# Scores a chunk ahead, values of the dilated heads first, seven products from chunk 3, and one x tile per row

## The chip, the core and the metric

The kernel runs on one core of a Trainium2 chip. A core has TensorE for matrix products, VectorE, ScalarE and GpSimd for element-wise work, a SyncE queue (SP) that issues most transfers, and 16 DMA engines behind the queues. The time is device microseconds from start to end of one launch; it is given as the median of several runs. A profile is taken of one execution by the hardware; its span runs from the first to the last instruction.

## What is computed

The inputs are q, k and v of shape (8, 8, 576, 64): 8 batch rows, 8 heads, 576 positions, 64 channels, in float32. Each row goes through attention with two masks, and the result through a feed-forward block:

```python
scores = (1 / sqrt(64)) * q @ k.T
rel = pos[:, None] - pos[None, :]
mask_plain = (rel >= 0) & (rel < 32)                        # heads 0 to 3, "sliding"
mask_dil = (rel >= 0) & (rel < 128) & (rel % 4 == 0)        # heads 4 to 7, "dilated"
attn = softmax(where(mask, scores, -1e9))
x = (attn @ v)  ->  (4608 tokens, 512)                      # 8 rows of 576 tokens
h = x @ w_in                                                # 512 -> 2048
out = relu(h) ** 2 @ w_out                                  # 2048 -> 512, float32
```

## The kernel before

**Two units of work.** Attention is done by batch row: eight rows b = 0 to 7 of 576 tokens. The feed-forward block is done by chunk: nine chunks c = 0 to 8 of 512 tokens (chunk 0 takes 576, chunk 1 the 448 behind them). A chunk is `mm1` (16 blocks of 128 of the 2048 inner columns; each is four accumulated matmuls over the 512 input columns, then a relu on ScalarE into `rt`; VectorE squares two blocks at a time into `g`) and then `mm2` (g times w_out). All is in float16 with float32 accumulation.

**The plain mm2 and the seven products.** `mm2_gen` runs 4 token blocks of 16 matmuls, 512 columns wide. `seven_gen` computes the same product of a chunk with seven products of half-size blocks instead of eight, 112 matmuls of 256 columns; it needs sums of parts of g (`S1` to `S3`, made on VectorE behind mm1 by `sums_behind` and once more in the products), sums of parts of w_out (`T1` to `T4`, made once by `sum_w_out_gen` in eight VectorE subtractions), and seven VectorE additions or subtractions at the end. Before, chunks 1 to 3 take the plain form and chunks 4 to 8 the seven products; the T sums are made during chunk 2.

**A row's attention** is cut into steps, named in `row_parts`: `s0`, `s1` scores of the sliding heads and `z0`, `z1` of the dilated heads (TensorE, then two exps on ScalarE, then one multiply by the mask on VectorE into `AT`); `a0` to `a2` values of the sliding heads and `d0`, `d1`, `e0`, `e1` of the dilated heads (eight small matmuls AT times v, then a reciprocal and a multiply on VectorE); `x0`, `x1`, `y0`, `y1` transposes of the result on TensorE and a ScalarE copy into `xT`, from which mm1 reads. The scores and values steps use four PSUM banks as two pairs in turn, the chunk's matmuls the other four.

**The order is written by hand.** A chunk is a generator with 64 steps (32 in mm1; 32 in the plain mm2, 28 in the seven products). `run` advances it and inserts the row's parts at given steps: "24:s0" puts s0 behind step 24. Each engine works its instructions in the order of the program. In chunk c the program works on row b = c + 1. Before, chunks 1 and 2 hold the scores of row b at steps 24 to 36 and its values at 40 to 60; chunk 3 holds the scores and values of row 4 at 2 to 20 and 24 to 44, and the scores of row 5 at 47 to 59; chunks 4 and 5 hold the values of row b at 2 to 32 and the scores of the row behind it at 36 to 54; chunk 6 the values of row 7.

**How a row's data come.** Ahead of chunk c the program issues, for row b + 1: on GpSimd a `see` (a one-element copy that waits until row b's `QKTp` has landed), two loads `n` (q and k of the sliding heads, cast to float16 on the way) and two `dd` (dilated heads, to a DRAM buffer); then the copy `o` of n into token order (`in_token_order`, 128 x 2304 elements). On SP: two transposing DMAs from dd into `QKTd`, two stores of o into a DRAM buffer `dp`, two transposing DMAs from dp into `QKTp`, and the loads of v: six of `sv` (sliding heads) and two of `sd` (dilated heads). GpSimd then casts row b's v from sv and sd into `vp` and `vd` (`cast_v`: three casts and four). sv and sd exist once, QKTp, QKTd, vp and vd twice, xT has room for three rows.

**xT** is one tile with a ring of three rows:

```python
RING = 3 * S
xT = const.tile([P, NDM, RING], FP16, name="xT")
```

`x_sliding` and `x_dilated` write row b at place b % 3, and `mm1_tile` reads 512 tokens from place t0 % RING, in two matmuls where the ring ends. That is so in chunk 3 (192 + 320) and in chunk 6 (384 + 128).

Of the kernel before, what the change touches and what calls it, by code (L numbers as in the profile page):

```python
# [8 lines left out]
FP16 = mybir.dt.float16  # L9
# [4 lines left out]
P = 128  # L14
# [3 lines left out]
def kernel(  # L18
# [9 lines left out]
    nc = tc.nc  # L28
# [56 lines left out]
        return b if dt == FP32 else b.bitcast(dt)  # L85


    RING = 3 * S
    xT = const.tile([P, NDM, RING], FP16, name="xT")


    WI = ((0, 512), (512, 1024), (1024, 2048))
# [60 lines left out]
    def load_sliding_v(b, m0=0, m1=NB):  # L153
        for m in range(m0, m1):
            lo = QB * m - PADP
            p0 = PADP if m == 0 else 0
            nc.sync.dma_start(
                out=sv[p0:P, m, :, :],
                in_=v[b, 0:HH, lo + p0 : lo + P, :].transpose([1, 0, 2]),
            )  # L160

    def load_dilated_v(b, t):
        vv = v[b, HH:H].rearrange("h (i c) d -> i h (c d)", c=DIL)
        if t:
            nc.sync.dma_start(out=sd[:, 1, :, :], in_=vv[QD - PADD : CL])
        else:
            nc.sync.dma_start(out=sd[PADD:P, 0, :, :], in_=vv[0:QD])

    def load_v(b):
        load_sliding_v(b)  # L170
        for t in range(2):
            load_dilated_v(b, t)

    def load_w_in(t):
        f0, f1 = WI[t]
# [24 lines left out]
    def cast_sliding_v(b, mp):  # L200
        m = 2 * mp
        nc.gpsimd.tensor_copy(vp[b % 2][:, m : m + 2, :, 0:D], sv[:, m : m + 2, :, :])  # L202

    def cast_dilated_v(b, t, a):
        c = 2 * a
        nc.gpsimd.tensor_copy(  # L206
            vd[b % 2][:, t, c : c + 2, :, 0:D],
            sd[:, t, :, D * c : D * (c + 2)].rearrange("p h (c d) -> p c h d", d=D),
        )

    def cast_v(b):
        for mp in range(NB // 2):
            cast_sliding_v(b, mp)
        for t in (0, 1):
            for a in range(2):
                cast_dilated_v(b, t, a)

# [7 lines left out]
            )  # L225
        return d

    def in_token_order(b, n):
        o = natp.tile([P, 9, HH, D], FP16, name=f"o{b}", tag="o")
        nc.gpsimd.tensor_copy(o, n.rearrange("p h j d -> p j h d"))  # L230
        return o

    def keep_sliding_qk(b, o):
# [18 lines left out]
    def mm1_tile(ffc, t0, t1, rt):  # L252
        w = t1 - t0
        ph = bank()
        o = t0 % RING
        cut = min(w, RING - o)
        for dmk in range(NDM):
            for a, b, x in ((0, cut, o), (cut, w, 0)):
                if a < b:
                    nc.tensor.matmul(  # L260
                        ph[:, a:b],
                        w_in_of(dmk, ffc),
                        xT[:, dmk, x : x + b - a],
                        start=(dmk == 0 and a == 0),
                        stop=(dmk == NDM - 1 and b == w),
                    )
            if dmk == 1:
                yield
        nc.scalar.activation(rt, ph[:, 0:w], ACTF.Relu)  # L269
# [394 lines left out]
    def x_sliding(b, half, xs, wide):  # L664
        px = pt(wide)
        for m3 in range(3):
            m = 3 * half + m3
            x = xs[m // 2][:, m % 2].rearrange("p h d -> p (h d)")
            for c in range(2):
                nc.tensor.transpose(  # L670
                    px[:, 288 * c + QB * m3 : 288 * c + QB * (m3 + 1)],
                    x[:, P * c : P * (c + 1)],
                    ident[0:QB, 0:QB],
                )
        t0 = (b % 3) * S + 288 * half
        nc.scalar.copy(  # L676
            xT[:, 0:2, t0 : t0 + 288],
            px[:, 0:UW].rearrange("x (c t) -> x c t", c=2),
        )

    def x_dilated(b, t, xs, wide):
        py = pt(wide)
        for a in range(2):
            for e in range(2):
                x = xs[a][:, e].rearrange("p h d -> p (h d)")
                for c in range(2):
                    o = 288 * c + QD * (2 * a + e)
                    nc.tensor.transpose(  # L688
                        py[:, o : o + QD],
                        x[0:QD, P * c : P * (c + 1)],  # L690
                        ident[0:QD, 0:QD],
                    )
        t0 = (b % 3) * S + 288 * t
        nc.scalar.copy(
            xT[:, 2:4, t0 : t0 + 288].rearrange("x c (i r) -> x c i r", r=DIL),
            py[:, 0:UW].rearrange("x (c r i) -> x c i r", c=2, r=DIL),
        )

# [199 lines left out]
    for t in range(2):  # L898
        for a in range(2):
            cast_dilated_v(1, t, a)  # L900
    o = in_token_order(2, n)
    transpose_dilated(2, dd)
    transpose_sliding(2, keep_sliding_qk(2, o))
    pending.append(mm2_by_rows_gen(0))
    parts = row_parts(1, True)
    parts.update(
# [7 lines left out]
            "4:t0 6:t1 8:s0:u0 10:s1:u1 12:z0 14:z1 18:a0 19:a1 20:a2 21:x0 22:d0 23:x1"  # L914
            " 24:d1 25:e0 26:e1 27:y0 28:y1",
            parts,
        )
    )
    load_v(2)

    rows_ = {b: row_parts(b, b > 3) for b in range(2, B)}
    SCORES = "{}:s0 {}:s1 {}:z0 {}:z1"
    VALUES = "{}:a0 {}:a1 {}:a2 {}:x0 {}:d0 {}:x1 {}:d1 {}:e0 {}:e1 {}:y0 {}:y1"
    for c in range(1, NTOKC):
        b = c + 1
        if b + 1 < B:
            see(QKTp[b % 2][0:1, 0, 0, PADP : PADP + 1])  # L930
            n, dd = load_whole_sliding_qk(b + 1), keep_dilated_qk(b + 1)
            o = in_token_order(b + 1, n)
            transpose_dilated(b + 1, dd)
            transpose_sliding(b + 1, keep_sliding_qk(b + 1, o))
        if b < B:
            cast_v(b)
        if b + 1 < B:
            load_v(b + 1)
        pending.append(moe_gen(c) if c < 4 else moe_seven_gen(c))
        plans, more = [], []  # L940
        if c < 3:
            plans.append((SCORES.format(*range(24, 40, 4)), rows_[b]))
            plans.append((VALUES.format(*range(40, 62, 2)), rows_[b]))
        if c == 2:
            it = sum_w_out_gen()
            more = [(4 + 7 * i, lambda it=it: next(it)) for i in range(8)]
        if c == 3:
            plans.append((SCORES.format(2, 8, 14, 20), rows_[b]))
            plans.append((VALUES.format(*range(24, 46, 2)), rows_[b]))
            plans.append((SCORES.format(47, 51, 55, 59), rows_[b + 1]))  # L950
        if 3 < c < B - 1:
            plans.append((VALUES.format(2, 5, 8, 11, 13, 16, 18, 22, 26, 29, 32), rows_[b]))
        if 3 < c < B - 2:
            plans.append((SCORES.format(36, 42, 48, 54), rows_[b + 1]))
        run(*plans, more=more)


# [28 lines left out]
```

## Time and profile before

| | |
|---|---|
| median of 3 runs | 312.45 us (312.25 to 313.09) |
| the profiled execution | 313.25 us, span 311.2 us |
| granted TensorE clock | 1.0 |
| TensorE busy | 297.2 us, 95% of the span, 2932 matmuls |
| VectorE busy | 198.2 us, 64% |
| ScalarE busy | 161.8 us, 52% |
| GpSimd busy | 85.4 us, 27% |
| starts of chunks 1 to 8 in the span | 65.6, 96.3, 128.6, 163.4, 194.9, 226.5, 255.5, 281.6 us |

In the profile PE is TensorE, DVE VectorE, ACT ScalarE, POOL GpSimd and SP the SyncE queue; L260 is a line of the kernel as printed above. L260 is mm1, L301 the plain mm2, L396 the seven products, L588 and L602 the scores, L641 and L655 the values, L670 and L688 the transposes, L676 and L694 the copies into xT. The chain of waits is followed back from the last instruction; each piece has its start in the span, its length, and the engine and line. A view by windows gives the busy time of each engine in a stretch of the span. In the timeline the bracket behind an instruction is the idle time of its engine ahead of it and what ended that.

### The profile page before, as it was taken

The page shows a single profiled execution, that of the slowest core. Times are in us where ns is not written, and L with a number is a line of the kernel's source. Part 1 is how long each engine was busy: PE and PEld are TensorE (multiplying, and loading weights), DVE is VectorE, ACT ScalarE, POOL GpSimd, SP SyncE. Part 2 cuts the span into 40 slices and gives each one's busy share as a digit, 9 for nine tenths or more (in the row PEclk, how much of TensorE's full clock was granted, in tenths as well). Part 3 has the DMA queues.
Part 4 walks back from the last instruction along what each step waited for, and adds up shares of the span by engine and source line. Part 5 has one row for each costly group of instructions (what it writes and reads, how often), then busy time and mean ns, then how long its engine had stood idle before and what let it go on. Part 6 is the DMA issues. An engine that isn't in the chain of part 4 may idle for free.

```text
span 311.2 us, 7133 instructions
## 1 busy us (share of the span) xinstructions
PE 297.2 (95%) x2932; PEld 200.7 (65%) x2932; DVE 198.2 (64%) x354; ACT 161.8 (52%) x286; POOL 85.4 (27%) x120
## 2 busy tenths in 40 slices
PE   3988999899999999999999999999999999999995
PEld 3657954455555555687545578657888885685584
DVE  6545645835852986297345879686868753863674
ACT  2646857278536772686356653565456406504610
POOL 5591027132703913283350344006000000000000
PEclk9999999999999999999999999999999999999999
DMA  7999989699979999998938894886120020012012
GB/s 117 242 205 212 213 185 234 156 227 206 224 180 220 266 196 164 248 235 166 236 134 185 162 216 122 190 173 141 67 71 3 2 101 34 2 46 91 0 36 101
DMA packets 75376, 46.73 MB, mean 150 GB/s; under 512 B 54416, under 2 KB 71056, under 8 KB 75152
## 3 DMA queue, kind: packets, MB, share of 16 engines
q1 hardware_dynamic: 67952, 32.52, 44.4%
q0 software_dynamic: 7248, 13.63, 24.7%
q8 instruction: 23, 0.38, 0.5%
q10 hardware_dynamic: 144, 0.13, 0.1%
q14 instruction: 9, 0.07, 0.1%
HBM read 39.85 MB, written 16.52 MB: 181 GB/s over the span
## 4 chain that ended last, share of the span: by engine, by line
PE 92%; DVE 2%; DMA 2%; ACT 2%; issue 1%; POOL 0%; DVEq 0%; POOLq 0%
PE PS L260 41%; PE PS L396 20%; PE PS L301 17%; PE PS L655 3%; PE PS L588 2%; PE PS L641 2%; PE PS L602 2%; DMA nd<-in_q_dram 2%; PE PS L688 1%; PE PS L670 1%; PE PS L523 1%; DVE AT L573 1%; ACT AT L569 1%; PE PS L581 1%; DVE x_p L627 1%
## 5 line engine op out<-in xcount | busy, mean ns | idle before, releaser
L260 PE MATMUL PS<-xT,wi 128*128 128x512 f16 (+6 forms) x768 | 136.1, 329 | 2.9 <-ACT xT L676 1.7
L269 ACT ACTIVATE rt<-PS 128x512 f16<-128x512 f32 (+2 forms) x160 | 88.7, 555 | 66.8 <-PE PS L260 64.0
L260 PEld LDWEIGHTS <-wi 128*128 128x128 f16 x768 | 79.2, 114 | 42.1 <-issue 3.0
L294 DVE TENSOR_TENSOR g<-rt 128x1024 f16<-128x1024 f16 (+1 forms) x64 | 47.6, 747 | 38.5 <-ACT rt L269 38.4
L301 PE MATMUL PS<-wo,g 128*128 128x512 f16 x256 | 64.4, 379 | 0.0
L569 ACT ACTIVATE AT<-PS 128x576 f16<-128x576 f32 x64 | 38.4, 650 | 19.8 <-PE PS L602 12.1
L396 PEld LDWEIGHTS <-S 128*128 128x128 f16 x320 | 31.0, 98 | 3.8
L301 PEld LDWEIGHTS <-g 128*128 128x128 f16 x256 | 21.3, 97 | 18.2
L396 PE MATMUL PS<-T,S 128*128 128x256 f16 x240 | 28.2, 273 | 0.0
L573 DVE TENSOR_TENSOR AT<-AT,maskp 128x1152 f16<-128x1152 f16 x14 | 15.0, 1072 | 19.1 <-ACT AT L569 19.1
L202 POOL CAST vp<-sv 128x512 f16<-128x512 f32 x24 | 20.6, 874 | 23.6 <-DMA sv<-in_v_dram 23.6
L206 POOL CAST vd<-sd 128x512 f16<-128x512 f32 x32 | 23.7, 773 | 10.5 <-DMA sd<-in_v_dram 10.4
L396 PEld LDWEIGHTS <-g 128*128 128x128 f16 x240 | 23.0, 98 | 3.2
L627 DVE TENSOR_TENSOR x_d<-PS,rcp_d 72x512 f16<-72x512 f32 x32 | 22.0, 687 | 1.1
L230 POOL COPY o<-n 128x2304 f16<-128x2304 f16 x6 | 13.0, 2172 | 30.6 <-issue 29.4
L396 PE MATMUL PS<-wo,g 128*128 128x256 f16 x160 | 19.5, 273 | 0.0
L676 ACT COPY xT<-PS 128x576 f16<-128x576 f16 x16 | 10.2, 637 | 14.6 <-PE PS L670 14.5
L573 DVE TENSOR_TENSOR AT<-AT,maskd 128x1152 f16<-128x1152 f16 x14 | 12.8, 917 | 7.3 <-ACT AT L569 7.3
L627 DVE TENSOR_TENSOR x_p<-PS,rcp_p 96x512 f16<-96x512 f32 x24 | 16.5, 687 | 0.8
L655 PEld LDWEIGHTS <-AT 128*128 128x128 f16 x256 | 12.4, 102 | 7.0 <-DVE x_d L627 1.3
L311 ACT COPY ot<-PS 128x512 f32<-128x512 f32 x16 | 9.4, 587 | 14.4 <-PE PS L301 14.4
L283 DVE TENSOR_TENSOR g<-rt 128x288 f16<-128x288 f16 x32 | 9.9, 309 | 9.9 <-ACT rt L269 9.8
(86 smaller groups left out, 257.3 us busy)
## 6 DMA issues: line engine op xcount, KB each, us to landing
sv<-in_v_dram SPq DMA_DIRECT2D x40, 128.0 KB, 4.0
out_dram<-c SPq DMA_DIRECT2D x19, 256.0 KB, 2.5
sd<-in_v_dram SPq DMA_DIRECT2D x8, 512.0 KB, 12.2
out_dram<-ot SPq DMA_DIRECT2D x15, 256.0 KB, 12.2
dp<-o SPq DMA_DIRECT2D x12, 288.0 KB, 3.8
sd<-in_v_dram SPq DMA_DIRECT2D x8, 288.0 KB
wo<-in_moe_w_out_dram POOLq DMA_DIRECT2D x4, 512.0 KB, 13.7
n<-in_k_dram POOLq DMA_DIRECT2D x6, 288.0 KB, 5.8
```

The costliest lines, as they stand in the source:

```text
L202: nc.gpsimd.tensor_copy(vp[b % 2][:, m : m + 2, :, 0:D], sv[:, m : m + 2, :, :])
L206: nc.gpsimd.tensor_copy(vd[b % 2][:, t, c : c + 2, :, 0:D], sd[:, t, :, D * c : D * (c + 2)].rearrange("p h (c d) -> p c h d", d=D),)
L230: nc.gpsimd.tensor_copy(o, n.rearrange("p h j d -> p j h d"))
L260: nc.tensor.matmul(ph[:, a:b], w_in_of(dmk, ffc), xT[:, dmk, x : x + b - a], start=(dmk == 0 and a == 0), stop=(dmk == NDM - 1 and b == w),)
L269: nc.scalar.activation(rt, ph[:, 0:w], ACTF.Relu)
L294: nc.vector.tensor_mul(g[:, f2 : f2 + 2, o:TOKC], rt[:, :, o:TOKC], rt[:, :, o:TOKC])
L301: nc.tensor.matmul(po, g[:, ffc, o + t * P : o + (t + 1) * P], w_out_of(ffc), start=(ffc == 0), stop=(ffc == NFF - 1),)
L396: nc.tensor.matmul(po[t], lhs(j)[:, t * P : (t + 1) * P], rhs(j), start=j == 0, stop=j == HF - 1)
L569: nc.scalar.activation(AT[:, u + i, 0:UW], ps[:, :, 0 : UW // 2], ACTF.Exp, scale=scale)
L573: nc.vector.tensor_mul(AT[:, u : u + n, 0:UW], AT[:, u : u + n, 0:UW], mask.unsqueeze(1).to_broadcast([P, n, UW]),)
L627: nc.vector.tensor_tensor(out=x[0:w], in0=pv[:, :, :, 0:D], in1=rcp[0:w].unsqueeze(3).to_broadcast([w, 2, HH, D]), op=ALU.mult,)
L655: nc.tensor.matmul(pav[:, e, h * (D + 2) : h * (D + 2) + D + 1], AT[:, 4 + 2 * a + t, off : off + P], vd[b % 2][:, t, 2 * a + e, h, 0 : D ...
```

## The change

It has five parts.

1. xT becomes three tiles, one for each place. `mm1_tile` now cuts a chunk wherever it crosses from one row to the next, not only at the ring's end: chunks 2 to 7 are cut (128 + 384, 192 + 320, 256 + 256, 320 + 192, 384 + 128, 448 + 64).
2. Chunk 3 takes the seven products too, and the T sums are made during chunk 1.
3. From row 4 on all four scores steps of a row come in the chunk in front, dilated heads first; row 3's scores and values come earlier in chunk 2; the values of rows 4 to 7 begin with the dilated heads, and in chunk 3 they lie at every third step.
4. From row 4 on, v of the dilated heads is loaded and cast first, and the casts of row b's v stand ahead of the o copy of row b + 1 on GpSimd.
5. The o copy of row 2 moves from GpSimd to ScalarE, at step 17 of chunk 0's mm2; the DMAs behind it are issued there too.

```diff
-    RING = 3 * S
-    xT = const.tile([P, NDM, RING], FP16, name="xT")
+    xT = [const.tile([P, NDM, S], FP16, name=f"xT{r}") for r in range(3)]
...
-    def load_v(b):
-        load_sliding_v(b)
+    def load_v(b, dilated_first=False):
+        if not dilated_first:
+            load_sliding_v(b)
         for t in range(2):
             load_dilated_v(b, t)
+        if dilated_first:
+            load_sliding_v(b)
...
-    def cast_v(b):
-        for mp in range(NB // 2):
-            cast_sliding_v(b, mp)
+    def cast_v(b, dilated_first=False):
+        if not dilated_first:
+            for mp in range(NB // 2):
+                cast_sliding_v(b, mp)
         for t in (0, 1):
             for a in range(2):
                 cast_dilated_v(b, t, a)
+        if dilated_first:
+            for mp in range(NB // 2):
+                cast_sliding_v(b, mp)
...
-    def in_token_order(b, n):
+    def in_token_order(b, n, eng=nc.gpsimd):
         o = natp.tile([P, 9, HH, D], FP16, name=f"o{b}", tag="o")
-        nc.gpsimd.tensor_copy(o, n.rearrange("p h j d -> p j h d"))
+        copy(eng, o, n.rearrange("p h j d -> p j h d"))
         return o
...
     def mm1_tile(ffc, t0, t1, rt):
         w = t1 - t0
         ph = bank()
-        o = t0 % RING
-        cut = min(w, RING - o)
+        rows_in = [(r, max(t0, r * S), min(t1, (r + 1) * S)) for r in range(t0 // S, (t1 - 1) // S + 1)]
         for dmk in range(NDM):
-            for a, b, x in ((0, cut, o), (cut, w, 0)):
-                if a < b:
-                    nc.tensor.matmul(
-                        ph[:, a:b],
-                        w_in_of(dmk, ffc),
-                        xT[:, dmk, x : x + b - a],
-                        start=(dmk == 0 and a == 0),
-                        stop=(dmk == NDM - 1 and b == w),
-                    )
+            for r, a, b in rows_in:
+                nc.tensor.matmul(
+                    ph[:, a - t0 : b - t0],
+                    w_in_of(dmk, ffc),
+                    xT[r % 3][:, dmk, a - r * S : b - r * S],
+                    start=(dmk == 0 and a == t0),
+                    stop=(dmk == NDM - 1 and b == t1),
+                )
...
-    o = in_token_order(2, n)
-    transpose_dilated(2, dd)
-    transpose_sliding(2, keep_sliding_qk(2, o))
+
+    def turn_row_2():
+        transpose_dilated(2, dd)
+        transpose_sliding(2, keep_sliding_qk(2, in_token_order(2, n, nc.scalar)))
+
     pending.append(mm2_by_rows_gen(0))
...
+        more=[(17, turn_row_2)],
...
-    rows_ = {b: row_parts(b, b > 3) for b in range(2, B)}
+    SEVEN = 3
+    rows_ = {b: row_parts(b, b > SEVEN) for b in range(2, B)}
     SCORES = "{}:s0 {}:s1 {}:z0 {}:z1"
     VALUES = "{}:a0 {}:a1 {}:a2 {}:x0 {}:d0 {}:x1 {}:d1 {}:e0 {}:e1 {}:y0 {}:y1"
+    SOON = "{}:z0 {}:z1 {}:s0 {}:s1"
+    EARLY = "{}:d0 {}:d1 {}:e0 {}:y0 {}:e1 {}:a0 {}:y1 {}:a1 {}:a2 {}:x0 {}:x1"
+    LATER = (EARLY.format(2, 5, 8, 11, 13, 16, 19, 21, 24, 27, 30), SOON.format(36, 42, 48, 54))
+    PLANS = {
+        1: (SCORES.format(*range(24, 40, 4)) + " " + VALUES.format(*range(40, 62, 2)), ""),
+        2: (
+            SCORES.format(8, 14, 20, 26) + " " + VALUES.format(*range(30, 52, 2)),
+            SOON.format(52, 56, 59, 62),
+        ),
+        3: (
+            EARLY.format(8, 11, 14, 17, 19, 22, 24, 27, 30, 33, 36),
+            SOON.format(40, 45, 50, 55),
+        ),
+        4: LATER,
+        5: LATER,
+        6: (LATER[0], ""),
+    }
     for c in range(1, NTOKC):
         b = c + 1
         if b + 1 < B:
             see(QKTp[b % 2][0:1, 0, 0, PADP : PADP + 1])
             n, dd = load_whole_sliding_qk(b + 1), keep_dilated_qk(b + 1)
+        if 3 < b < B:
+            cast_v(b, True)
+        if b + 1 < B:
             o = in_token_order(b + 1, n)
             transpose_dilated(b + 1, dd)
             transpose_sliding(b + 1, keep_sliding_qk(b + 1, o))
-        if b < B:
+        if b <= 3:
             cast_v(b)
         if b + 1 < B:
-            load_v(b + 1)
-        pending.append(moe_gen(c) if c < 4 else moe_seven_gen(c))
-        plans, more = [], []
-        if c < 3:
-            plans.append((SCORES.format(*range(24, 40, 4)), rows_[b]))
-            plans.append((VALUES.format(*range(40, 62, 2)), rows_[b]))
-        if c == 2:
+            load_v(b + 1, b + 1 > 3)
+        pending.append(moe_gen(c) if c < SEVEN else moe_seven_gen(c))
+        more = []
+        if c == 1:
             it = sum_w_out_gen()
-            more = [(4 + 7 * i, lambda it=it: next(it)) for i in range(8)]
-        if c == 3:
-            plans.append((SCORES.format(2, 8, 14, 20), rows_[b]))
-            plans.append((VALUES.format(*range(24, 46, 2)), rows_[b]))
-            plans.append((SCORES.format(47, 51, 55, 59), rows_[b + 1]))
-        if 3 < c < B - 1:
-            plans.append((VALUES.format(2, 5, 8, 11, 13, 16, 18, 22, 26, 29, 32), rows_[b]))
-        if 3 < c < B - 2:
-            plans.append((SCORES.format(36, 42, 48, 54), rows_[b + 1]))
-        run(*plans, more=more)
+            more = [(2 + 3 * i, lambda it=it: next(it)) for i in range(8)]
+        now, ahead = PLANS.get(c, ("", ""))
+        run((now, rows_.get(b)), (ahead, rows_.get(b + 1)), more=more)
```

More of the change, by code (lines that the diff above doesn't have):

```diff
@@ L674, in x_sliding @@
                 )
-        t0 = (b % 3) * S + 288 * half
+        t0 = 288 * half
         nc.scalar.copy(
-            xT[:, 0:2, t0 : t0 + 288],
+            xT[b % 3][:, 0:2, t0 : t0 + 288],
             px[:, 0:UW].rearrange("x (c t) -> x c t", c=2),
@@ L692, in x_dilated @@
                     )
-        t0 = (b % 3) * S + 288 * t
+        t0 = 288 * t
         nc.scalar.copy(
-            xT[:, 2:4, t0 : t0 + 288].rearrange("x c (i r) -> x c i r", r=DIL),
+            xT[b % 3][:, 2:4, t0 : t0 + 288].rearrange("x c (i r) -> x c i r", r=DIL),
             py[:, 0:UW].rearrange("x (c r i) -> x c i r", c=2, r=DIL),
@@ L916 @@
             parts,
-        )
+        ),
+        more=[(17, turn_row_2)],
     )
     load_v(2)
-    rows_ = {b: row_parts(b, b > 3) for b in range(2, B)}
+    SEVEN = 3
+    rows_ = {b: row_parts(b, b > SEVEN) for b in range(2, B)}
     SCORES = "{}:s0 {}:s1 {}:z0 {}:z1"
     VALUES = "{}:a0 {}:a1 {}:a2 {}:x0 {}:d0 {}:x1 {}:d1 {}:e0 {}:e1 {}:y0 {}:y1"
+    SOON = "{}:z0 {}:z1 {}:s0 {}:s1"
[10 more added lines that the diff above has]
+            SOON.format(40, 45, 50, 55),
+        ),
+        4: LATER,
+        5: LATER,
+        6: (LATER[0], ""),
+    }
     for c in range(1, NTOKC):
```

## Prediction, made before the result was known

> **What bounds the kernel now.** I read the page first, then the chain of waits in order of time, then the windows by chunk, and last the timeline of each place where the chain leaves TensorE. The page's busy rows and the head of its chain:
>
> ```profile
> PE 297.2 (95%) x2932; PEld 200.7 (65%) x2932; DVE 198.2 (64%) x354; ACT 161.8 (52%) x286; POOL 85.4 (27%) x120
> PE 92%; DVE 2%; DMA 2%; ACT 2%; issue 1%; POOL 0%; DVEq 0%; POOLq 0%
> ```
>
> TensorE is busy 95% and carries 92% of the chain, at a granted clock of 1.0. So a gain is either TensorE work that goes away or one of the few places where it stands still. From the chain in order of time, three kinds of line price the work:
>
> ```profile
> 126.90 1.73 PE PS L301 x8
> 269.35 12.23 PE PS L396 x112
> 154.20 0.36 PE PS L588 x12
> 154.56 1.83 PE PS L301 x8
> 204.41 1.73 PE PS L260 x8
> 236.15 1.75 PE PS L260 x16
> ```
>
> Eight 512-wide matmuls take 1.73 us (0.2166 each), so 64 take 13.86, for mm1 and for the plain mm2 alike; the seven products of a chunk take 12.23. One scores step takes 0.36, and the eight matmuls behind it 1.83 instead of 1.73, so 0.47 in all, and four take 1.88. A values step (8 or 6 matmuls) adds 0.25 to 0.26 between its neighbours, eleven 2.8. The last two lines are mm1 of chunk 5 (whole) and chunk 6 (each 512 cut into 384+128 where the ring wraps): 0.02 more for eight pairs. With these prices the chunks come out: chunk 2 13.86+13.86+1.88+2.8 = 32.4, and the chain has 32.3 (96.27 to 128.6); chunk 4 13.86+12.23+1.88+2.8 = 30.8 against 31.4; chunk 5 30.8 against 31.6; chunk 3 with eight score steps 14.0+13.9+3.8+2.8 = 34.5 against 34.8. What is left over in 3, 4 and 5 are waits, and row 1's values in chunk 0 hold another. The timeline (start, duration, engine, line):
>
> ```profile
> 53.62 2.11 POOL L230 COPY o<-n 128x2304 f16<-128x2304 f16 x1 [1.22 <-DMA n<-in_q_dram]
> 54.07 2.27 DVE L573 TENSOR_TENSOR AT<-AT,maskd 128x1152 f16<-128x1152 f16 x1 [0.94 <-ACT AT L569]
> 57.23 0.43 PE L641 MATMUL PS<-vp,AT 128*128 128x65 f16 x8 [1.09 <-DVE x_p L627]
> 178.34 0.38 PE L260 MATMUL PS<-xT,wi 128*128 128x512 f16 x1
> 179.24 1.24 PE L260 MATMUL PS<-xT,wi 128*128 128x512 f16 x5 [0.51 <-ACT xT L694]
> 210.66 1.46 PE L260 MATMUL PS<-xT,wi 128*128 128x512 f16 x6 [0.73 <-ACT xT L694]
> ```
>
> The mask multiply that takes 0.76 at 52.36 takes 2.27 beside GpSimd's copy, and a2 waits behind it. In chunks 4 and 5 a matmul of mm1 waits for the copy of y0, which writes the next row, a row that this chunk does not read.
>
> **Row 2's o copy on ScalarE (chunk 0, step 17).** Removed: the 2.27 beside the copy; the multiply goes back to 0.76 and ends at 54.83, so x of a0 (0.20+0.69 and gaps) is there at 55.95 instead of 57.17. a1 starts at 55.29 and steps follow each other by 0.69, so a2 starts at 55.98 instead of 57.23. Then VectorE's pace (0.93 a step) binds: x of a1 56.89, of a2 57.82, d0 at 57.85 instead of 58.90. I take -1.05. Added: one ScalarE copy of 2304 elements. The rows 288 (0.410), 448 (0.546) and 576 (0.650) give 0.83 ns an element on 0.17, so 2.1 us as an estimate (those read PSUM; the copy reads SBUF). It starts when the exps end (54.03) and n has landed (53.62), ends near 56.1, and the next ScalarE work, x0's copy, comes at 57.3: hidden by 1.2 us. Behind it wait only that copy and, on SP, dp's stores, which start at 58.01 after the dilated transposes anyway. Bounds: -1.25, and 0 if the copy took over 3 us.
>
> **sum_w_out one chunk earlier.** Eight subtractions of 0.68 to 0.69 (those beside GpSimd's work took up to 2.59) at steps 2 to 23 of chunk 1. Three steps are 1.13 us, with 0.68+0.47 of VectorE work: full, but chunk 1 has no other VectorE work till step 24, and three rt buffers cover the lag. Nothing on the path; without that cover, at most the lag of some 0.5 us. Chunk 2 loses them and gets row 4's four masks (0.75 to 1.16 each): about even.
>
> **Seven products in chunk 3.** TensorE: 13.86 becomes 12.23, -1.63. VectorE gets 8 sums and 7 combinations of 0.69 (10.4 us), ScalarE loses four copies of 0.58 and gets one. In the windows, chunk 4 now does all of this with VectorE under four fifths busy:
>
> ```profile
> 128.60:163.40 34.80, 34.80 (x390) 23.18 (x388) 20.19 (x30) 22.80 (x40) 18.47 (x21) 1.00 0.85 196
> 163.40:194.85 31.45, 30.94 (x318) 21.74 (x316) 24.42 (x40) 17.63 (x30) 9.38 (x13) 1.00 0.78 170
> ```
>
> (Columns: length, then busy us of PE, PEld, DVE, ACT, POOL, clock, DMA share, GB/s.) Chunk 3 is harder, because GpSimd's casts lie over its mm1 and a 0.69 g multiply takes 1.09 there: some five of them and a mask or two, +2 to 3 us, about 27 of 31. Zero stall; with a full rt ring 1 to 2 us.
>
> **Scores one chunk in front, values spread.** Row 4's scores move whole from chunk 3 to chunk 2: +1.88 and -1.88. Row 3's earlier steps change no work. Chunk 3's values go from every second step to every third: the two waits for x there (142.44+0.88 to 143.73 holds 0.43 where 0.25 is due, and the same at 147.99) go, -0.34. Data for row 4's scores: the look at 119.10 shows its sliding transposes landed; s0 at step 59 of chunk 2 comes near 127. Cover 8 us.
>
> **x in a tile per row.** A copy for the next row no longer shares a tile with what mm1 reads. In chunk 4, 178.34+0.22 to 179.24 is 0.68; in chunk 5, y0 at 209.51 plus 0.25 to 210.66 is 0.89. Together -1.57; nothing is late next, because the copies' readers come a chunk later. But every chunk that crosses a row is now cut: 2, 4, 5 and 7 are new (128+384, 256+256, 320+192, 448+64), 3 and 6 were cut already. From the two L260 lines, 0.02 for eight is 0.16 a chunk, 0.64 for four. A 64-wide matmul streams in 27 ns, but eight 65-wide ones take 0.25 to 0.26 us, 32 ns each: +0.32 in chunk 7. Sum +0.96; between 0 and 5.5 (64 times the 113 ns of a weight load, less 27); I take the 65-wide row, nearest in width and with the same weights.
>
> Against the cut speaks the Trainium skill, "TensorE: Matmul & The Clock Gate", section "Back-to-back issue gap": in a stream of load-and-matmul pairs a 128-wide matmul needs about 81 ns. An estimate by that page: 28 ns more on 64 pieces in chunk 2 and at least 54 more on 64 in chunk 7, 5.2 us and with 0.32 for chunks 4 and 5 5.5, and the change would give back all it saves and end near 313.4. The trace differs: the 384+128 pairs of chunk 6 take 218 ns, of which 160 are the 384's.
>
> **Casts ahead of copies, dilated first (GpSimd and SP).** Same instructions, same DMAs, other order. On SP sd (two DMAs) passes the six of sv; on GpSimd seven casts (3.8+3.2 us) pass the o copy (2.1). Behind them wait o, then dp, then the sliding transposes of the next row. Row 4: sd issued at about 115.2, its longest landing in the trace is 13.5, so 128.7, first cast 129.6; d0 at step 8 of chunk 3 is due near 133. Casts end near 136, o 138, dp's two stores 139.4, landing 3.8, transposes 143 to 146: row 5's s0, step 50, is due at 155. Row 5: sd issued at 145.7, landed by 158 at 12.2, first cast 158.8; d0, step 2 of chunk 4, due near 161. So nothing on the path, with 2 to 3 us to spare at the tightest. Rows 6 and 7 have more, DMA being quieter there.
>
> **Sum.** -1.05 -1.63 -0.34 -1.57 +0.96 = -3.63 us. The profiled execution was 313.25 (span 311.2, 2.05 around it), 0.8 over the median; that one should become 309.6, the span 307.6, and the median 312.45 becomes 308.8. What a measurement of this kernel can tell from no change is about 0.3%, 0.94 us, so "same" is 311.5 to 313.4.
>
> **Rivals.** (a) The ring of GpSimd and DMA sets the pace, and it ends slower. By the order above each row's sd follows its transposes, and the next row's transposes follow sd's casts: 12.2 landing + 3.8 + 3.2 casts + 2.1 copy + 1.2 + 3.8 dp + 3.2 transposes = 29.5 us, against a chunk of 30.9. At a landing of 16 us row 5's d0 is 1.6 late and rows 6 and 7 each 2.4 more: +6.4, in all +2.8, 315.2. The whole gain is gone from a landing of about 15. For it: DMA is 0.85 and 0.78 busy there, and d0, in order on TensorE, stops all of mm1. Against: 13.5 is the longest seen, and sd goes first now. 0.12. (b) The same or VectorE's load in chunk 3 costs 1.5 to 2.5 once: 310.3 to 311.3. 0.13. (c) The waits on xT stay, since they were not the tile's: 308.8+1.57 = 310.4. For it: x1's copies, in the same tile, stop nothing. Against: the matmul's releaser is that copy itself, and no other data links them. 0.05. (d) Stalls and cuts together leave it within 0.3%: 0.05.
>
> **How the numbers follow.** The forecast, 307.8 (no cost of cuts, -4.6) to 310.0 (the o copy's gain lost), has 0.65. Faster: forecast, (b) and (c), 0.83; same 0.05; slower 0.12. The range 307.5 to 311.3 leaves out (a), (d) and a little below.
>
> **What would show it.** Right: 3236 matmuls (2932 -64 +112 +256); the mask multiply near 54 at 0.8; a2 near 56; no L260 waiting on L694 in chunks 4 and 5; chunk 3 close to 31 us, chunk 7's mm1 13.8 to 14.3; span near 307.6. Wrong: d0 (L655) waiting on GpSimd's vd at the start of chunk 4 or 5; s0 or z0 waiting on a transpose; relus waiting on VectorE in chunk 3; chunk 7's mm1 above 15.

## The result, and the profile after

The changed kernel takes 310.49 us in the median (309.37 to 311.68, 8 runs) against 312.35 before (311.53 to 313.89, 8 runs): the ratio is 0.9931, with a 95% interval of 0.9902 to 0.996. Run once more beside other kernels it took 310.26 against 313.43, 0.9908 (0.9876 to 0.994). The profiled execution took 310.64 us, its span is 308.9. So the kernel is faster: the first interval is 1.2 to 3.1 us, the second 1.9 to 3.9. The 3.6 that were counted lie outside the first and inside the second. The time, 310.49, lies above the forecast of 307.8 to 310.0 and inside the wider range up to 311.3, near its upper part.

The lines of the page that answer to those of before, the busy rows and the head of the chain:

```profile
PE 294.0 (95%) x3236; PEld 222.0 (72%) x3236; DVE 208.4 (67%) x369; ACT 161.9 (52%) x284; POOL 81.5 (26%) x119
PE 76%; DMA 11%; POOL 5%; DVE 4%; issue 1%; ACT 1%; SPq 1%; POOLq 0%; DVEq 0%; ACTq 0%
```

The 3236 matmuls are there. TensorE still carries most of the chain, but GpSimd, VectorE and transfers now have a fifth of it. Part of that is the start: this chain goes back through row 2's n to the first transfers. The other part is new waits in chunks 0, 2 and 3.

The price is best read by stages. I took the first matmul of each stage from the timeline, and the times between them; the start of a run (to chunk 0's first mm2 matmul) is kept apart, because it varies from 39.6 to 42.0 us over the executions below, whatever the kernel:

| kernel | start | mm2 of chunk 0 | chunk 2 | chunk 3 | chunk 4 | chunk 5 | chunk 7 | span without the start |
|---|---|---|---|---|---|---|---|---|
| before | 40.70 | 24.74 | 32.37 | 34.79 | 31.43 | 31.64 | 26.04 | 270.46 |
| changed | 39.63 | 24.47 | 35.65 | 31.32 | 30.94 | 30.93 | 26.43 | 269.23 |
| changed_again | 40.21 | 24.07 | 35.20 | 32.09 | 30.94 | 30.93 | 26.43 | 269.13 |
| rowtwo_on_gpsimd | 42.02 | 23.51 | 34.92 | 31.54 | 30.94 | 30.93 | 26.43 | 267.82 |
| no_row3_casts | 39.93 | 24.32 | 34.45 | 31.46 | 30.94 | 30.92 | 26.43 | 267.99 |
| row3_casts_first | 41.36 | 24.22 | 35.95 | 31.79 | 30.93 | 30.93 | 26.43 | 269.71 |
| one_xT_ring | 41.83 | 24.25 | 34.91 | 30.92 | 30.93 | 30.93 | 26.45 | 267.84 |
| ring_uncut | 40.66 | 23.71 | 34.67 | 31.54 | 32.10 | 32.54 | 26.04 | 270.07 |
| before_row_cut | 39.89 | 23.47 | 32.90 | 34.79 | 32.62 | 30.92 | 26.44 | 272.70 |
| row3_scores_early | 41.74 | 23.47 | 34.45 | 30.92 | 30.94 | 30.93 | 26.43 | 266.62 |
| all_mended | 40.23 | 23.65 | 34.64 | 30.92 | 30.94 | 30.93 | 26.04 | 268.19 |
| early_whole | 40.51 | 24.66 | 34.45 | 30.92 | 30.95 | 30.93 | 26.04 | 267.41 |
| early_whole_gpsimd | 41.37 | 23.52 | 34.45 | 30.92 | 30.95 | 30.93 | 26.04 | 266.27 |
| plain_chunk3 | 40.79 | 23.63 | 35.20 | 33.01 | 30.93 | 30.93 | 26.43 | 269.60 |

Chunks 1, 6 and 8 are the same within 0.1 us in all, but for chunk 1 in before_row_cut (32.73) and all_mended (32.25), where it is 30.7 elsewhere. Of the 2.30 us by which the span fell from the first row to the second, 1.07 are the start, which by the other rows is chance; 1.23 are left. That is the difference of two executions, and of the unedited kernel before there is only this one. Chunks 4, 5 and 7 did what was counted. Chunk 0's mm2, chunk 2 and chunk 3 did not. The timeline of the changed kernel at these three places (start, duration, engine, line; the bracket is the idle time ahead and what ended it):

```profile
52.91 0.76 DVE L577 TENSOR_TENSOR AT<-AT,maskd 128x1152 f16<-128x1152 f16 x1 [0.94 <-ACT AT L573]
55.63 2.11 ACT L198 COPY o<-n 128x2304 f16<-128x2304 f16 x1 [2.75 <-DMA n<-in_q_dram]
57.65 0.63 ACT L680 COPY xT<-PS 128x576 f16<-128x576 f16 x1
58.33 0.42 PE L674 MATMUL PS<-ident,x_p 96*128 96x96 f16 x6 [0.92 <-ACT xT L680]
...
103.28 2.10 POOL L200 COPY o<-n 128x2304 f16<-128x2304 f16 x1 [5.72 <-issue]
103.29 2.71 DVE L577 TENSOR_TENSOR AT<-AT,maskp 128x1152 f16<-128x1152 f16 x1 [1.27 <-ACT AT L573]
105.33 3.17 POOL L204 CAST vp<-sv 128x512 f16<-128x512 f32 x3
105.92 2.11 DVE L298 TENSOR_TENSOR g<-rt 128x1024 f16<-128x1024 f16 x2
107.96 1.16 DVE L577 TENSOR_TENSOR AT<-AT,maskd 128x1152 f16<-128x1152 f16 x1
112.39 0.69 DVE L631 TENSOR_TENSOR x_p<-PS,rcp_p 96x512 f16<-96x512 f32 x1
113.13 0.43 PE L645 MATMUL PS<-vp,AT 128*128 128x65 f16 x8 [0.89 <-DVE x_p L631]
...
133.45 2.56 POOL L200 COPY o<-n 128x2304 f16<-128x2304 f16 x1
134.76 1.80 DVE L298 TENSOR_TENSOR g<-rt 128x1024 f16<-128x1024 f16 x1 [0.71 <-ACT rt L273]
137.45 0.43 PE L659 MATMUL PS<-vd,AT 128*128 128x65 f16 x8 [0.23 <-DVE x_d L631]
```

In chunk 0 the mask multiply is free (0.76), but n lands at 55.6, so ScalarE stands for 2.75 us and then copies for 2.11, and x0's copy waits its turn behind it; x1 needs x0's pair of banks. In chunk 2 a mask multiply begins 0.01 us after GpSimd's copy and takes 2.71; the g multiplies behind it run beside the casts at 1.05 and the masks at 1.16, and a2 waits for x of a0 (the multiply `x_p`), which stands behind them all on VectorE. In chunk 3 the next o copy meets a g multiply (1.80), with d0's normalization behind it and e0 behind that.

The page of the Trainium skill "SBUF — State Buffer", section "Who interferes with whom", says that a VectorE instruction with two SBUF inputs contends with a GpSimd instruction that reads SBUF, that the port pair they share is an exclusive lock, and that a VectorE instruction with at most one SBUF input, outside the two-port modes, does not contend. The rows agree: the copy ends at 103.28 + 2.10 = 105.38, and the mask multiply, which takes 0.76 alone, is done 0.62 later; and in rowtwo_on_gpsimd the multiply x_p, which has one input in PSUM, takes its usual 0.69 at 57.41 in the midst of the copy that began at 56.98.

### The profile page after: what moved, and what is told of

Its sections match the earlier page's. It is cut to its first block, busy times and chain, and to the rows that moved or that the text cites. A ratio compares the mean times of both kernels' runs of the same rounds, so it can differ in the third digit from the quotient of the medians.

```text
span 308.9 us, 7741 instructions
## 1 busy us (share of the span) xinstructions
PE 294.0 (95%) x3236; PEld 222.0 (72%) x3236; DVE 208.4 (67%) x369; ACT 161.9 (52%) x284; POOL 81.5 (26%) x119
## 4 chain that ended last, share of the span: by engine, by line
PE 76%; DMA 11%; POOL 5%; DVE 4%; issue 1%; ACT 1%; SPq 1%; POOLq 0%; DVEq 0%; ACTq 0%
PE PS L264 32%; PE PS L400 24%; PE PS L305 10%; DMA wo<-in_moe_w_out_dram 5%; DMA ns<-in_q_dram 2%; PE PS L659 2%; DMA n<-in_q_dram 2%; DVE g L298 2%; DVE AT L577 2%; PE PS L645 1%; PE PS L592 1%; PE PS L692 1%; PE PS L674 1%; PE PS L606 1%; DMA sv<-in_v_dram 1%
## 5 line engine op out<-in xcount | busy, mean ns | idle before, releaser
L264 PE MATMUL PS<-xT,wi 128*128 128x288 f16 (+8 forms) x1024 | 136.0, 286 | 1.5 <-ACT xT L680 1.5
L264 PEld LDWEIGHTS <-wi 128*128 128x128 f16 x1024 | 96.9, 114 | 27.1 <-issue 0.8
L298 DVE TENSOR_TENSOR g<-rt 128x1024 f16<-128x1024 f16 (+1 forms) x64 | 51.1, 800 | 36.6 <-ACT rt L273 36.1
L305 PE MATMUL PS<-wo,g 128*128 128x512 f16 x192 | 48.9, 379 | 0.0
L400 PEld LDWEIGHTS <-S 128*128 128x128 f16 x384 | 37.0, 98 | 4.6
L400 PE MATMUL PS<-T,S 128*128 128x256 f16 x288 | 34.1, 273 | 0.0
L204 POOL CAST vp<-sv 128x512 f16<-128x512 f32 x24 | 18.2, 769 | 25.7 <-DMA sv<-in_v_dram 25.3
L400 PE MATMUL PS<-wo,g 128*128 128x256 f16 x192 | 23.4, 273 | 0.0
L190 POOL COPY look<-QKTp 1x1 f16<-1x1 f16 x5 | 1.7, 345 | 55.1 <-DMA QKTp<-dp 55.1
L680 ACT COPY xT<-PS 128x576 f16<-128x576 f16 x16 | 10.2, 638 | 8.8 <-PE PS L674 8.4
L659 PE MATMUL PS<-vd,AT 128*128 128x65 f16 x256 | 13.8, 197 | 0.2 <-DVE x_d L631 0.2
```

The lines of the kernel that those rows point to most:

```text
L264: nc.tensor.matmul(ph[:, a - t0 : b - t0], w_in_of(dmk, ffc), xT[r % 3][:, dmk, a - r * S : b - r * S], start=(dmk == 0 and a == t0), stop ...
L298: nc.vector.tensor_mul(g[:, f2 : f2 + 2, o:TOKC], rt[:, :, o:TOKC], rt[:, :, o:TOKC])
L305: nc.tensor.matmul(po, g[:, ffc, o + t * P : o + (t + 1) * P], w_out_of(ffc), start=(ffc == 0), stop=(ffc == NFF - 1),)
L400: nc.tensor.matmul(po[t], lhs(j)[:, t * P : (t + 1) * P], rhs(j), start=j == 0, stop=j == HF - 1)
L659: nc.tensor.matmul(pav[:, e, h * (D + 2) : h * (D + 2) + D + 1], AT[:, 4 + 2 * a + t, off : off + P], vd[b % 2][:, t, 2 * a + e, h, 0 : D ...
L680: nc.scalar.copy(xT[b % 3][:, 0:2, t0 : t0 + 288], px[:, 0:UW].rearrange("x (c t) -> x c t", c=2),)
```

## The experiments

**Row 2's o copy back on GpSimd.**

```diff
-    def turn_row_2():
-        transpose_dilated(2, dd)
-        transpose_sliding(2, keep_sliding_qk(2, in_token_order(2, n, nc.scalar)))
+    o = in_token_order(2, n)
+    transpose_dilated(2, dd)
+    transpose_sliding(2, keep_sliding_qk(2, o))
...
-        more=[(17, turn_row_2)],
```

> Row 2's o copy back on GpSimd, at its old place; all else as changed. In the changed kernel the stretch from chunk 0's first mm2 matmul to chunk 1's first mm1 matmul took 24.5 us, before 24.75. Theory (the ScalarE copy traded one wait for another: x1's transposes waited 0.92 for x0's copy, which stood behind the o copy): x1's wait goes; the wait of a2 comes back only if the copy meets z1's mask multiply, that is if n lands before that multiply is done. So the stretch is about 24.75 with the mask multiply at 2.2 us, or about 23.7 with it at 0.76; the whole kernel between the same and +0.4 us of the changed one, or 0.8 below it. Rival (the ScalarE copy did win its 1.05 us and something else in this stretch took it): the stretch is 25.3 or more, and x1 still waits.

Measured: 310.26 us, ratio to before 0.9892 (0.9833 to 0.9952); chunk 0's mm2 took 23.51. x1's wait is gone, and the copy came after z1's mask:

```profile
55.29 1.13 DVE L577 TENSOR_TENSOR AT<-AT,maskd 128x1152 f16<-128x1152 f16 x1 [0.62 <-ACT AT L573]
56.98 2.11 POOL L200 COPY o<-n 128x2304 f16<-128x2304 f16 x1 [1.17 <-DMA n<-in_q_dram]
57.41 0.69 DVE L631 TENSOR_TENSOR x_p<-PS,rcp_p 96x512 f16<-96x512 f32 x1
```

That is the theory's second case for this stretch; the 0.8 us that it gave for the whole kernel do not show in the median. The rival (ScalarE had won its 1.05) falls. The execution profiled before the change, with n landed at 53.6 and the copy on the mask, was the bad case of its own place: in three later executions with the copy on GpSimd the stretch took 23.5.

**Row 3's casts left out.**

```diff
-        if b <= 3:
+        if b <= 2:
             cast_v(b)
```

> The seven casts of row 3's v in chunk 2 are left out (row 3's values are then computed with row 1's v). In the changed kernel chunk 2 took 35.7 us where 34.4 was counted; a2 waited 0.89 for x of a0, and VectorE's multiplies took 1.0 to 2.7 us there instead of 0.7. Theory (GpSimd's o copy and casts at 103 to 113 us hold up the mask and g multiplies, now that row 3's masks lie there too): with only the 2.1 us copy left, the g and mask multiplies behind it go back to 0.7 and 0.76, a2 does not wait, chunk 2 is 34.3 to 34.6. Rival (VectorE simply has too much work between step 8 and step 34, whatever GpSimd does): chunk 2 stays at 35.5 or more and a2 waits 0.7 or more.

Measured: 309.69 us in one run; chunk 2 took 34.45 us, 0.04 from the 34.41 counted (32.37, four scores steps at 1.88, the cut at 0.16), and a2 did not wait:

```profile
104.14 2.60 POOL L200 COPY o<-n 128x2304 f16<-128x2304 f16 x1 [6.71 <-issue]
...
105.44 1.85 DVE L298 TENSOR_TENSOR g<-rt 128x1024 f16<-128x1024 f16 x1 [0.66 <-ACT rt L273]
107.22 0.74 DVE L577 TENSOR_TENSOR AT<-AT,maskd 128x1152 f16<-128x1152 f16 x1
109.63 0.76 DVE L577 TENSOR_TENSOR AT<-AT,maskd 128x1152 f16<-128x1152 f16 x1 [1.07 <-ACT AT L573]
```

Behind the copy the multiplies are back at 0.7. VectorE has time enough for its own work; the rival falls.

**Row 3's casts ahead of the copy.**

```diff
-        if 3 < b < B:
-            cast_v(b, True)
+        if 2 < b < B:
+            cast_v(b, b > 3)
...
-        if b <= 3:
+        if b <= 2:
             cast_v(b)
```

> Row 3's casts stand ahead of row 4's o copy on GpSimd (in the order sliding, dilated), as from row 4 on in the changed kernel. Theory (GpSimd over the masks): GpSimd's work of chunk 2 starts near 98 instead of 103 and ends near 109 instead of 113; VectorE has caught up by step 34; chunk 2 is 34.4 to 35.1 and the kernel 0.6 to 1.2 us faster than the changed one. Row 4's sliding transposes land 3 to 5 us later, near 124, due at 127. Rival (too much work on VectorE): chunk 2 unchanged at 35.7. Rival (the chain of row 4's transposes binds): s0 of row 4 waits and chunk 2 is longer than 35.7.

Measured: 311.96 us, ratio 0.9953 (0.992 to 0.9986); chunk 2 took 35.95, longer than in the changed kernel, and a2 waited more. This was a miss, and all three theories as stated fall:

```profile
110.67 2.11 POOL L200 COPY o<-n 128x2304 f16<-128x2304 f16 x1
...
110.96 2.43 DVE L577 TENSOR_TENSOR AT<-AT,maskd 128x1152 f16<-128x1152 f16 x1 [1.27 <-ACT AT L573]
...
114.88 0.43 PE L645 MATMUL PS<-vp,AT 128*128 128x65 f16 x8 [1.20 <-DVE x_p L631]
```

sd landed only at 107.1, so the copy came at 110.7, upon the last mask multiply ahead of the values. One multiply held up shortly ahead of a0 was enough for the whole loss; that GpSimd's casts came earlier did not help. s0 of row 4 did not wait.

**One ring for xT, cuts kept.**

```diff
-    xT = [const.tile([P, NDM, S], FP16, name=f"xT{r}") for r in range(3)]
+    xT = const.tile([P, NDM, 3 * S], FP16, name="xT")
...
-                    xT[r % 3][:, dmk, a - r * S : b - r * S],
+                    xT[:, dmk, (r % 3) * S + a - r * S : (r % 3) * S + b - r * S],
...
```

> xT as one tile with a ring of three rows; the cuts at the rows and all else as changed. Theory (a copy into the shared tile holds up mm1's reads of other rows): after y0, a matmul of mm1 waits for the copy again in chunks 4 and 5 (0.7 to 0.9 each) and perhaps after y0 or y1 in chunks 3 and 6, where they too lie in mm1 now; the kernel 1.4 to 3 us slower than the changed one. Rival (the waits came from the ring's place in step order, not from the tile): no such wait, same time within 0.3 us.

Measured: 311.48 us, ratio 0.9952 (0.9919 to 0.9984); chunks 4 and 5 took 30.93 each, and no matmul of theirs waits for a copy. The theory falls: where mm1 is cut, the tile per row does nothing. (The median is 1.0 above the changed kernel's, but the intervals of both overlap; in the profiled execution no stage is longer, chunks 2 and 3 are shorter, and the start is 2.2 us longer.) But the edit left the new cuts in place.

**The ring with the old cut, and the kernel before with the new cut.**

```diff
-        rows_in = [(r, max(t0, r * S), min(t1, (r + 1) * S)) for r in range(t0 // S, (t1 - 1) // S + 1)]
+        o = t0 % (3 * S)
+        cut = min(w, (3 * S) - o)
         for dmk in range(NDM):
-            for r, a, b in rows_in:
+            for a, b, x in ((0, cut, o), (cut, w, 0)):
...
```

> The changed kernel with the ring and the old cut, at the ring's end alone; so chunks 2, 4, 5 and 7 read 512 columns across a row's border in one matmul. With the ring and the new cuts chunks 4 and 5 took 30.93 us each, like the changed kernel. Theory (a matmul that reads across a row's border is tied to the copies of y0 and y1 into a third row; the cut undoes the tie, the tile per row does nothing): in the program two matmuls of chunk 4 and two of chunk 5 wait for a y copy, each 0.5 to 0.9 us on TensorE, so these chunks take 31.8 to 32.4; chunk 7 takes 26.04 and chunk 2's mm1 is 0.1 to 0.2 shorter. Rival (the waits of the kernel before came from the late place of y0 in mm1): chunks 4 and 5 take 30.8 with no such wait.

Measured: 312.5 us in one run; chunk 4 took 32.10 and chunk 5 32.54. The waits are back, twice in each. Its waits (who waits, for whom, total us, times, longest):

```profile
PE PS L266 <- ACT xT L700: 2.5, 4, 0.7
```

Its timeline in chunk 4, where the second group of matmuls waits 0.51 us for the copy:

```profile
167.01 0.38 PE L266 MATMUL PS<-xT,wi 128*128 128x512 f16 x1
167.91 0.81 PE L266 MATMUL PS<-xT,wi 128*128 128x512 f16 x3 [0.51 <-ACT xT L700]
```

The other way round, with the cut at row borders put into the kernel before:

> The kernel before with one edit: mm1 is cut at row borders, in the ring as it was. Theory (the cut alone takes the two waits away): chunk 4 takes 30.8 to 30.9 us instead of 31.43 and chunk 5 30.8 to 30.9 instead of 31.64; chunk 7 takes 26.43 instead of 26.04, chunk 2 about 0.1 more; all in all -0.8 us on the span beside what the start of the run varies by. Rival (the order of values and the tile matter too): a wait of 0.5 us or more on y0's copy stays in chunk 4 or 5.

Measured: 314.67 us in one run. mm1 of chunk 4 went from 17.32 to 16.81 and chunk 5 from 31.64 to 30.92: both waits are gone with the cut alone. The total went the other way, by two waits in other places (two rows of its waits, then two of GpSimd's timeline):

```profile
PE PS L639 <- POOL vp L202: 1.9, 1, 1.9
PE PS L394 <- DVE c L448: 1.5, 1, 1.5
...
79.67 2.10 POOL L230 COPY o<-n 128x2304 f16<-128x2304 f16 x1 [5.12 <-issue]
81.72 1.70 POOL L202 CAST vp<-sv 128x512 f16<-128x512 f32 x2
```

The first is a0 of row 2 in chunk 1. Its cast did not wait for v: it stood on GpSimd behind row 3's o copy, which began 16.3 us into the chunk instead of 10.2, because the loads and transposes of rows 2 and 3 had landed late. The second is a product of chunk 4, behind a mask multiply of 2.66 us that met the o copy of that chunk at 187.1. So the kernel before also loses to GpSimd's copy in some executions and not in others. In both directions cutting is what frees mm1 from the copies: a matmul whose 512 columns cross a row's border waits for the copy of another row, and the same columns read in two matmuls do not. Why the uncut read is tied to that copy, no run here tells.

**Row 3's scores early.**

```diff
         2: (
-            SCORES.format(8, 14, 20, 26) + " " + VALUES.format(*range(30, 52, 2)),
+            SOON.format(4, 8, 12, 16) + " " + VALUES.format(*range(30, 52, 2)),
```

> The changed kernel, but row 3's scores in chunk 2 come at steps 4, 8, 12 and 16, dilated heads first, instead of 8, 14, 20 and 26. Leaving out row 3's casts took chunk 2 to 34.45 us, the price that was counted; putting them ahead of the copy took it to 35.95, since the copy then met the last mask multiply ahead of the values. Theory (what costs is a mask multiply beside GpSimd's copy or casts shortly ahead of a0): the four masks are done near 104, before or at the start of the copy, g alone is left beside the casts, and VectorE is clear by step 30; chunk 2 takes 34.4 to 34.8. Rival (g multiplies at 1.05 beside the casts are enough to hold up a0 to a2): chunk 2 takes 35.2 or more. Rival (row 3's sliding transposes, landed near 95 to 97, come too late for s0 at step 12): TensorE waits ahead of L592.

Measured: 310.12 us in one run with a late start (41.74); without the start 266.62 us, 2.6 below the changed kernel. Of these 1.2 are chunk 2; chunk 0 gave 1.0, which varies without this edit too, and chunk 3 gave 0.4, which comes in all four executions with this edit. Chunk 2 took 34.45, and chunk 3 30.92 without a wait:

```profile
104.00 0.76 DVE L577 TENSOR_TENSOR AT<-AT,maskp 128x1152 f16<-128x1152 f16 x1 [0.39 <-ACT AT L573]
...
105.12 2.10 POOL L200 COPY o<-n 128x2304 f16<-128x2304 f16 x1 [6.98 <-issue]
...
105.14 2.63 DVE L298 TENSOR_TENSOR g<-rt 128x1024 f16<-128x1024 f16 x1 [0.39 <-ACT rt L273]
107.69 1.17 DVE L577 TENSOR_TENSOR AT<-AT,maskp 128x1152 f16<-128x1152 f16 x1
```

The copy now meets a g multiply, and the last mask is done at 108.9, 2 us ahead of a0. Both rivals fall. No scores step waited for a transpose.

**Three mends together.** Early scores; chunks 2 and 7 read whole from the ring; row 2's o copy at step 24, with row 2's dilated transposes issued ahead of it, at their old place:

```diff
+        if t0 // TOKC in (2, 7):
+            rows_in = [(t0 // S, t0, t1)]
...
+    transpose_dilated(2, dd)
+
     def turn_row_2():
-        transpose_dilated(2, dd)
         transpose_sliding(2, keep_sliding_qk(2, in_token_order(2, n, nc.scalar)))
...
-        more=[(17, turn_row_2)],
+        more=[(24, turn_row_2)],
```

> The changed kernel with three edits: row 3's scores early as in row3_scores_early; the ring with cuts at the rows in chunks 3 to 6 only (chunk 2 and 7 whole); row 2's o copy on ScalarE at step 24 instead of 17, behind the copies of x0 and x1. Theory: chunk 0's mm2 takes 23.5 to 23.7 us instead of 24.2 to 24.5 (x1 no longer waits for x0's copy), chunk 2 34.3 to 34.7, chunks 4 and 5 30.93, chunk 7 26.04; 2 us below the changed kernel, near 308.5. Rival (the later o copy pushes row 2's and row 3's transposes past their scores): TensorE waits ahead of L592 in chunk 1 (step 24) or chunk 2 (step 12), and the gain is under 1 us.

Measured: 310.32 us, ratio 0.9885 (0.9825 to 0.9945). The 308.5 of the theory was missed. Chunk 0's mm2 (23.65), chunks 2 and 7 are as expected, but chunk 1 lost 1.6:

```profile
82.95 0.42 PE L647 MATMUL PS<-vp,AT 128*128 128x65 f16 x8 [1.43 <-POOL vp L204]
```

The copy ended 2.7 us ahead of chunk 1 instead of 6.4, and the stores into dp followed at once; so row 2's sliding transposes landed later, GpSimd, which waits for them ahead of row 3's loads, went on at 71.3 instead of 69.4, and row 3's copy came at 79.7 instead of 77.8. Row 2's casts stand behind that. The rival was right that the delay would be paid, wrong about where. (In before_row_cut the same wait came with the copy at its old place, from n that landed late; so the late copy is one way to it, and a late landing is another.)

**Early scores and whole chunks, with the copy at its place, on either engine; the changed kernel again; the plain chunk 3.** The first is the ring with the edits of the last diff but step 24, the second has the edit of rowtwo_on_gpsimd besides.

> The changed kernel with two edits: row 3's scores at steps 4, 8, 12 and 16 of chunk 2, dilated heads first, and the ring with chunks 2 and 7 read whole (cuts in 3 to 6 only). Row 2's o copy stays on ScalarE at step 17. Counted behind the start of chunk 0's mm2, where the run's own start no longer matters, the kernel before took 270.5 us, the changed one 269.2, and with the early scores alone 266.6. Theory: 266.0 to 266.8 here, chunk 2 34.2 to 34.5, chunk 7 26.04; 2.0 to 2.6 us below the changed kernel in the median. Rival (the gains of the single runs were the luck of when transfers landed): the median is within 0.8 us of the changed kernel's, and a wait for a cast, a copy or a transpose stands in another chunk.

> As early_whole, with row 2's o copy on GpSimd, as before the change. Theory (the two places lose in opposite cases: GpSimd's copy holds up z1's mask when n lands ahead of it, 24.74 us for chunk 0's mm2 in the kernel before against 23.5 in two later executions; ScalarE's holds up x0's copy when n lands late, 24.2 to 24.5 against 23.5 to 23.7): the median is within 0.6 us of early_whole, on either side. Rival (ScalarE is the better place): 0.7 us or more above early_whole.

> The changed kernel once more, beside the mended ones. Theory: chunk 2 takes 34.9 to 35.7 us by where GpSimd's copy falls on the masks, chunk 0's mm2 23.5 to 24.5 by when n lands; median 1.5 to 3 us below the kernel before. Rival (its chunk 2 of 35.65 was a single bad execution): chunk 2 34.5 or less.

Measured on the same chip: early_whole 309.49 us, ratio 0.9867 (0.9835 to 0.9899); early_whole_gpsimd 309.54, 0.9868 (0.9829 to 0.9907); changed_again 310.26, 0.9908 (0.9876 to 0.994). The stages are as the theory has them: chunk 2 34.45 and chunk 7 26.04 in both, no wait in chunk 3. Without the start they are 1.7 and 2.9 us below changed_again. But the medians differ by 0.8, less than the 2.0 to 2.6 that I expected and as little as the rival named, and the intervals overlap: that these beat the changed kernel is shown for the stages, not for the median. As the rival has it, a wait stood elsewhere: early_whole lost 0.9 in chunk 0, this time since two mask multiplies met the casts of row 1's vd (3.81 for both), and its 267.41 without the start lies above the 266.0 to 266.8 expected. The two places of row 2's copy come out alike, as expected.

In changed_again chunk 2 took 35.20, inside the range expected, and its rival falls. The copy met no mask here but a g multiply, and the two dilated masks still took 1.16 each beside the casts: it is how far VectorE lags at a0 that costs, whichever multiply the copy meets. Chunk 3 took 32.09, for the o copy again:

```profile
134.38 2.10 POOL L200 COPY o<-n 128x2304 f16<-128x2304 f16 x1
...
134.46 2.57 DVE L298 TENSOR_TENSOR g<-rt 128x1024 f16<-128x1024 f16 x1 [1.05 <-ACT rt L273]
...
137.92 0.43 PE L659 MATMUL PS<-vd,AT 128*128 128x65 f16 x8 [1.00 <-DVE x_d L631]
```

```diff
-        pending.append(moe_gen(c) if c < SEVEN else moe_seven_gen(c))
+        pending.append(moe_gen(c) if c < 4 else moe_seven_gen(c))
```

> The changed kernel with the plain mm2 in chunk 3; all steps as changed. Theory (the seven products are worth 1.63 us on TensorE, and VectorE's 10 us more of work cost nothing): chunk 3 takes 32.5 to 33.0 us instead of 30.9 to 31.5. Rival (VectorE's extra work held up chunk 3 and ate part of it): chunk 3 at 32.2 or less.

Measured: 312.16 us in one run; chunk 3 took 33.01, of which mm1 16.80. Its second part is 16.21 us, and 14.62 in the changed kernel: the seven products are worth 1.59. Just above the range given for the theory, and the rival falls.

## Why the prediction was right in sign and too large

That the median fell inside the range is in part luck. The forecast proper ended at 310.0; the range went on to 311.3 for rivals (b), 310.3 to 311.3, and (c), 310.4, and neither came as it was put. What was missing came from three terms of the sum.

**Right.** The seven products: 1.63 counted, 1.59 measured. The moved scores, the values and the other TensorE work: chunk 2 comes to 34.45 where GpSimd is out of the way, against 34.41. The cuts: +0.39 in chunk 7 against 0.48, 6 ns a pair, and 0.16 in chunk 2 (mm1 16.43 cut, 16.27 whole) as counted, 2.5 ns a pair. The Trainium skill, "TensorE: Matmul & The Clock Gate", section "Back-to-back issue gap", gives about 81 ns for a 128-wide matmul in a stream of load-and-matmul pairs; in the 128 + 384 pairs of chunk 2 that figure does not hold. The order of casts and loads: no d0 waited for vd in any run of the changed kernel, and rival (a), the one that would have ended slower, did not come; sd, now first, was there 5 us after its issue (118.3, cast at 123.3), where I had allowed 13.5; the landings of sd in that execution are 5.3 to 7.0 us.

**Right in size, wrong in cause: x in a tile per row.** Chunks 4 and 5 lost 0.49 and 0.71, as -1.57 with the cuts' cost of 0.32 has it. But rival (c) had its point: not the tile but the cut did it (one_xT_ring, ring_uncut, before_row_cut). I had booked the cuts as a mere cost of the tiles. One matmul reads one tile, so a tile per row without the cuts could not be run.

**Wrong: "I take -1.05" for row 2's copy.** Chunk 0's mm2 gave 0.27. The copy's length was estimated rightly (2.1, measured 2.11). The cover named for it, 1.2 us until x0's copy, was read from one execution in which n landed at 53.6; it landed at 55.6 in the next. And the 2.27 us multiply was itself such a coincidence: with the copy on GpSimd the stretch took 24.74, 23.51, 23.47 and 23.52 in four executions, with it on ScalarE at step 17 between 23.47 and 24.66 in nine, 24.1 in the mean against 23.8. These runs show no gain from this part of the change.

**Wrong: that chunk 2, which loses the sums of w_out and gets row 4's masks, comes out "about even".** The sum of VectorE's work even fell (23.3 us before, 21.0 after, by the windows); its place was wrong. I had seen that row 3's scores moved 10 to 16 steps forward and wrote "Row 3's earlier steps change no work"; it put row 3's masks into the 10 us of GpSimd's copy and casts, with the values right behind. Price: 0.5 to 1.24 us over the five executions with the program of the changed kernel in this chunk (34.91, 34.92, 35.20, 35.20, 35.65).

**Wrong: "Zero stall" in chunk 3, and -0.34 for its old waits.** In the same executions chunk 3 with seven products took 30.92 to 32.09, on 30.94 counted (34.79 less 1.88, 1.63 and 0.34). Rival (b) named the place and put 1.5 to 2.5 on it; the mechanism is again one o copy that meets one g multiply, with d0's normalization behind it. Over all executions of the table with seven products there, the g multiply ahead of that normalization begins 4.32 us into the chunk. Where the copy began ahead of it (3.0 to 4.3 us in, five executions), the multiply took 1.8 to 2.6 us and the chunk 31.3 to 32.1; where the copy began later (4.7 to 6.8 us in), the chunk took 30.92 in five, and 31.46 in no_row3_casts, where the next g multiply was met (2.36).

Together the three misses are 0.78 + 1.24 + 0.38 = 2.40 us in the profiled execution, which is what lies between the counted 3.63 and the 1.23 read there. The medians need not agree with that pair of executions: chunk 0 of the one before was a bad case by 1.2 us, and other waits of the kernel before, like those in before_row_cut, come and go. How the whole gain divides on the average is not shown.

## What to carry to other kernels

Where two engines hold each other up, a sum of busy time per chunk says too little: look which instruction of the one stands next to which of the other, what is queued behind it and how soon that is needed, and move the one that others wait for. A stall read from one execution is worth its price only if the transfer that times it lands alike in the next; look for the same stretch in several profiles before booking it. And when an edit has a wanted part and a "cost" that comes with it, undo them one at a time: here the cost was the cause.

## What the runs showed that I had not expected

The start of a run, to the first mm2 matmul, varies from 39.6 to 42.0 us between executions, 2.4 us, more than the 1.9 that lie between the first two medians. A 64-wide matmul beside a 448-wide one costs only 6 ns more than its share of a 512-wide one, with its own weight load of 128 columns (3236 loads for 3236 matmuls). And in this program a read that crosses from one row's part of a tile to the next waited on a write to a third part, 0.7 to 0.9 us each time, where the same read in two pieces did not.
